# Hash products of the two column halves on the upper and the lower 64 rows of the array, with the projection laid out on the host

## The chip, the cores and the metric

The kernel is one program on one core of a Trainium2 chip. The metric is the device time of one execution in microseconds (us); the smaller the better. Engines are called PE (TensorE, the matrix array), DVE (VectorE), ACT (ScalarE), POOL (GpSimd) and SP (SyncE). DMA transfers are issued from the queues of SP, ACT and POOL.

## The reference

Three layers follow one another: a hash-bucketed attention (2 batches, 8 heads, 768 positions, head width 64), a top-2 mixture of 8 experts (1536 tokens, width 512, hidden width 1024) and a dense two-layer network (hidden width 2048). The change touches only the first. Cut to what matters:

```python
q_bits = (np.einsum('bhsd,dk->bhsk', q, proj) > 0)      # proj: 64 x 6
k_bits = (np.einsum('bhsd,dk->bhsk', k, proj) > 0)
mask = q_bucket[:, :, :, None] == k_bucket[:, :, None, :]   # bucket = the six bits as a number
scores = np.where(mask, scale * q @ k.T, -1e9)
attn = softmax(scores); out = attn @ v
```

Each position of q and k is multiplied by `proj`, the signs of the six products are its hash, and only positions with the same hash attend to each other.

## The kernel before, in words

The 16 heads are taken in 8 pairs (n = 0 to 7, j = 0 or 1 inside a pair). The host hands over q and k transposed, with the 64 rows of a head stacked twice, so that a tile `raw` (`rawq` and `rawk` in the profile) has 128 rows and 768 columns, and rows 64 to 127 repeat rows 0 to 63. The attention runs in 96 iterations g, 12 for each pair. In an iteration PE computes the scores of block g+2 (L277, `a_score`), DVE takes their maximum (L289, `a_soft`), PE transposes the probabilities of block g in two halves of three transposes (L319, `a_trans`), each half into one of two PSUM buffers of the tag "p", each half is copied out by ACT (L248) or DVE (L254), ACT computes the exponentials of block g+2 (L300, `a_exp`), and in every second iteration PE multiplies the transposed probabilities by v (L330, `a_av`). What else a pair needs is put into a table by iteration (`at`, and `at_m` for work that uses the single PSUM buffer of the tag "m"; `at_m` moves on to the next iteration in which no such work stands). Each engine runs its instructions in the order in which they are written out. Function `copy` chooses ACT or DVE for a copy by a ledger of the time that it has given to each.

The hash of a pair n >= 1 is `a_hash(n, hf)`, one call for each half of 384 columns, in two iterations: g0 - 2 and g0 - 1, where g0 is 7, 15, 29, 40, 50, 60 and 71 for n = 1 to 7 (the iterations come out as 5 and 6, 13 and 14, 27 and 28, 38 and 39, 48 and 49, 58 and 59, 69 and 70). A call makes four products (q and k of the two heads), each of `projq` (128 rows, of which rows 64 to 127 are zero, and 32 columns) with 384 columns of `raw`, into partitions 0, 32, 64 and 96 of the one "m" buffer. DVE then makes bits of them (L188) and scales half of these (L252, through `copy`). In iteration g0 `a_split` begins: ACT makes `u` (L169), POOL issues a transfer (L170) and subtracts (L171; on DVE for n = 1, j = 0), and so on for three more parts; `a_bits` then issues four transfers on POOL's queue (L197, L198) that bring the bits to the operands of the scores. `a_xt` (L364 to L375, a "m" user) transposes finished outputs, and the routing of finished tokens (`r_do`) is spread over iterations too. `w_conv` (L692 on ACT, L700 on POOL) prepares expert weights in iterations 28, 36, ... 68.

For pair 0 `z_hash(j)` does the same at the very start (L230), two products for each half, the second half in the buffer "av", and DVE reads the bits directly (L234).

`projq` is cleared by DVE and then filled by a transfer on POOL's queue (L65 to L68), which writes the six columns twice into rows 0 to 63. After it POOL issues `sgn`. ACT's queue carries `rawk` of head 0 at that time (L136), and ACT loads its table next (L494).

Of the kernel before, what the change touches and what calls it, by code (L numbers as in the profile page):

```python
# [9 lines left out]
F32 = mybir.dt.float32  # L10
F32R = mybir.dt.float32r
# [4 lines left out]
ALU = mybir.AluOpType  # L16
# [4 lines left out]
B, H, S, D = 2, 8, 768, 64  # L21
# [5 lines left out]
NB = 6  # L27
NROW = 24
HALF = 384
# [11 lines left out]
class Kernel:  # L41
# [19 lines left out]
    def consts(self):  # L61
        nc, a = self.nc, self.a
        p = self.cpool
        self.projq = self.t(p, [128, 32], F32, "projq")
        nc.vector.memset(self.projq, 0.0)  # L65
        src = a["proj"]
        src = bass.AP(tensor=src.tensor, offset=src.offset, ap=[[NB, 64], [0, 2], [1, NB]])
        nc.gpsimd.dma_start(self.projq[0:64, 0:2 * NB].rearrange("p (r b) -> p r b", r=2), src)  # L68
        self.sc = self.t(p, [128, 2], F32, "sc")
        nc.vector.memset(self.sc, 1.0)  # L70
        nc.vector.memset(self.sc[0:64, 0:1], SCALE)
        nc.vector.memset(self.sc[64:128, 1:2], SCALE)
        self.sgn = self.t(p, [128, 1], F32, "sgn")
        nc.gpsimd.dma_start(self.sgn, a["sgn"])
        self.ident = self.t(p, [128, 128], F32, "ident")
        make_identity(nc, self.ident)
# [97 lines left out]
            nc.scalar.activation(v1, k, AF.Copy, scale=self.sc[:, 1:2])  # L174
            eng.tensor_tensor(v2[0:64, :], k[0:64, :], v1[0:64, :].bitcast(F32), op=ALU.subtract)

    def a_hash(self, n, hf):
        nc = self.nc
        raw = self.raw[n]
        if hf == 0:  # L180
            self.hb[n] = self.t(self.ap, [128, S], F32R, "hb", 1)
        ps = self.t(self.ps_m, [128, HALF], F32, "m")
        cs = slice(hf * HALF, (hf + 1) * HALF)
        for i, (nm, j) in enumerate((("q", 0), ("q", 1), ("k", 0), ("k", 1))):
            nc.tensor.matmul(ps[32 * i:32 * i + 32, :], self.projq, raw[nm, j][:, cs],
                             start=True, stop=True)
        hb = self.hb[n][:, cs]
        nc.vector.tensor_scalar(hb, ps, 0.0, self.sgn[:, 0:1], op0=ALU.is_gt, op1=ALU.add)  # L188
        self.use(dve=0.47)
        self.copy(hb[64:128, :], hb[64:128, :].bitcast(F32), 0.4, 0.3, BIG)  # L190

# [30 lines left out]
    def z_hash(self, j):  # L222
        nc = self.nc
        u1, v1, u2, v2 = self.uv[0, j]
        pss = []
        for hf in range(2):
            cs = slice(hf * HALF, (hf + 1) * HALF)
            ps = self.t(*((self.ps_m, [128, HALF], F32, "m") if hf == 0 else (self.ps_a, [128, HALF], F32, "av")))
            for r, nm in ((64, "k"), (0, "q")):
                nc.tensor.matmul(ps[r:r + 32, :], self.projq, self.raw[0][nm, j][:, cs], start=True, stop=True)  # L230
            pss.append((ps, cs))
        def bits(h, d, r):
            ps, cs = pss[h]
            nc.vector.tensor_scalar(d[64:76, cs], ps[r:r + 12, :], 0.0, self.sgn[r:r + 12, 0:1], op0=ALU.is_gt, op1=ALU.add)  # L234
            if r == 0:
                nc.scalar.activation(d[64:76, cs], d[64:76, cs].bitcast(F32), AF.Copy, scale=BIG)

        for x in ((0, u2, 0), (0, v2, 64), (1, v2, 64), (1, u2, 0)):
            bits(*x)
# [251 lines left out]
    def attention(self):  # L491
# [3 lines left out]
        nc = self.nc  # L495
        LA = 2
        ps = self.t(self.ps_s, [128, 2, 512], F32, "s")
# [20 lines left out]
        self.at(0, self.a_load, 1)  # L518
        for n in range(1, NP):
            g = {1: 7, 2: 15, 3: 29, 4: 40, 5: 50, 6: 60, 7: 71}.get(n, 12 * (n - 1) - 2)  # L520
            h1 = self.at_m(g - 2, self.a_hash, n, 0)
            h1 = self.at_m(h1 + 1, self.a_hash, n, 1)
            self.at(g, self.a_uv, n)
            self.at(g, self.a_split, n, 0, 0)
            self.at(max(g, h1), self.a_bits, n)
            for x in range(1, 4):
                self.at(g + x, self.a_split, n, x // 2, x % 2)
            self.at(12 * n - 5, self.a_loadv, n)
            if n + 1 < NP:
                self.at(g + 4, self.a_load, n + 1)  # L530
# [16 lines left out]
        for bq, sc in ((0, 64), (1, 75)):  # L547
            g = xt[6 + bq] + 1
# [4 lines left out]
            g = self.at_m(g, self.r_do, bq, "rank", "place")  # L553
# [4 lines left out]
        for g in range(G):  # L558
            u, s, n, qh, j, c = self.dec(g)
# [748 lines left out]
def layout(inp):  # L1308
    import numpy as np
    c = np.ascontiguousarray  # L1310
    w64 = []
    w = c(inp["moe2_w_in"]).view(np.int64).reshape(4, 128, 2, 1024).transpose(2, 0, 1, 3).reshape(8, 128, 1024)
    w64.append(w)
    w = c(inp["moe2_w_out"]).view(np.int64).reshape(8, 2, 128, 512).transpose(0, 2, 1, 3).reshape(8, 128, 1024)
    w64.append(w)
    sgn = np.zeros((128, 1), np.float32)
    for g in range(4):
        for r in range(2 * NB):
            first = r < NB
            sgn[32 * g + r, 0] = -1.0 if first == (g >= 2) else 0.0  # L1320
    return {
        "qT": np.concatenate([inp["q"].transpose(0, 1, 3, 2)] * 2, axis=2),
        "kT": np.concatenate([inp["k"].transpose(0, 1, 3, 2)] * 2, axis=2),
        "v2": c(inp["v"].reshape(B, H // 2, 2, S // 128, 128, D).transpose(0, 1, 4, 3, 2, 5)).reshape(B, H // 2, 128, S // 128, 2 * D),
        "proj": inp["proj"], "sgn": sgn,
        "w_gate": inp["moe_w_gate"], "w_noise": inp["moe_w_noise"], "noise": inp["moe_noise"],
        "w1": inp["moe_w1"].reshape(E, 4, 128, FF),
        "w2": c(inp["moe_w2"].reshape(E, 4, 2, 128, DM).transpose(0, 1, 3, 2, 4)).reshape(E, 4, 128, 2 * DM),
        "w64": c(np.concatenate(w64)),
    }  # L1330
# [18 lines left out]
```

## Time and profile before

| | |
|---|---|
| median of 3 runs | 903.77 us (903.59 to 907.82) |
| profiled execution, its own time | 900.86 us |
| its span, first to last instruction | 899.1 us |
| mean granted clock of PE | 0.988 of full speed |
| attention | about 0 to 280 us of the span |

A profile shows one execution. Its page gives each engine's busy time; its chain of waits goes back from the last instruction to whatever released each step; the timeline lists instructions by start and duration, with the idle time before them and what ended it in square brackets. Full speed of PE is 2.4 GHz, the lower level 1.2 GHz. A full-precision product shows as two records, one behind the other.

### The profile page before, as it was taken

How to read it: one execution, taken by the hardware profiler on the slowest of the kernel's cores; microseconds unless marked ns; L12 is line 12 of the kernel's file. 1: busy time of each engine (PE TensorE's matmuls, PEld its weight loads, DVE VectorE, ACT ScalarE, POOL GpSimd, SP SyncE). 2: the span in 40 equal slices, each digit the busy share in tenths (PEclk: the TensorE clock that was granted, in tenths of full speed). 3: DMA queues.
4: the chain of work that ended last, by engine and by line, in shares of the span. 5: the costliest groups of instructions: out<-in, count | busy, mean ns of one | idle time of the engine just before them, and what ended most of it. 6: DMA issues, size and time to landing. Idle time of an engine off the chain costs nothing.

```text
span 899.1 us, 14065 instructions
## 1 busy us (share of the span) xinstructions
PE 867.4 (96%) x5409; PEld 747.7 (83%) x5409; DVE 539.3 (60%) x1079; ACT 439.4 (49%) x781; POOL 216.8 (24%) x222
## 2 busy tenths in 40 slices
PE   7999899989999999999999999999999999999997
PEld 4667666656667999999999999987989898989896
DVE  6676677897765568989898888837712121212120
ACT  5677777768774354435444343537614141414130
POOL 4142524565402300000000000005715050514040
PEclk9899999999999999999999999999999999999999
DMA  3428954744315756968787786748410101010000
GB/s 98 131 61 223 245 177 110 228 108 137 98 37 183 252 192 222 290 215 264 248 269 237 246 260 219 223 146 290 141 58 21 51 21 51 16 56 1 24 1 26
DMA packets 63016, 132.05 MB, mean 147 GB/s; under 512 B 8832, under 2 KB 25152, under 8 KB 62944
## 3 DMA queue, kind: packets, MB, share of 16 engines
q1 hardware_dynamic: 54240, 108.69, 37.9%
q0 software_dynamic: 7024, 20.38, 7.6%
q10 hardware_dynamic: 1680, 2.03, 0.7%
q8 instruction: 44, 0.72, 0.3%
q14 instruction: 28, 0.23, 0.1%
HBM read 91.90 MB, written 35.39 MB: 142 GB/s over the span
## 4 chain that ended last, share of the span: by engine, by line
PE 81%; DVE 6%; ACT 4%; DMA 4%; issue 2%; POOL 2%; SPq 0%; ACTq 0%; DVEq 0%; POOLq 0%
PE y L842 6%; PE y L844 5%; PE y L843 5%; PE g L1076 5%; PE g L1075 5%; PE g L1077 5%; PE av L330 5%; PE h L818 5%; PE h L819 5%; PE h L820 5%; PE o L1121 4%; PE o L1123 4%; PE o L1122 4%; PE s L277 4%; PE p L319 4%
## 5 line engine op out<-in xcount | busy, mean ns | idle before, releaser
L300 ACT ACTIVATE P<-s,sm 128x768 f32<-128x768 f32 x96 | 95.4, 994 | 35.0 <-DVE sm L291 29.5
L289 DVE TENSOR_REDUCE mx<-s 128x1 f32<-128x768 f32 x96 | 91.5, 954 | 24.7 <-PE s L277 23.7
L1085 POOL TENSOR_TENSOR gl<-sg,gh 128x512 fp32r<-128x512 f32 x48 | 67.2, 1400 | 162.1 <-ACT gh L1084 162.1
L277 PE MATMUL s<-v,u 76*128 76x384 f32 (+1 forms) x384 | 95.7, 371 | 5.8 <-ACT P L300 3.0
L1030 POOL DMA_INDIRECT yg<-ys,ysl x24 | 24.3, 1012 | 311.4 <-issue 309.1
L277 PEld LDWEIGHTS s<-v,u 76*128 76x128 f32 (+1 forms) x384 | 64.7, 195 | 35.8 <-issue 15.7
L319 PE MATMUL p<-ident,P 128*128 128x128 f32 x576 | 83.2, 280 | 10.4 <-DVE hh L254 4.5
L1081 DVE TENSOR_TENSOR sg<-g,sg 128x512 f32<-128x512 f32 x48 | 33.2, 691 | 91.1 <-ACT sg L1080 86.8
L319 PEld LDWEIGHTS p<-ident,P 128*128 128x128 f32 x576 | 70.0, 144 | 18.7 <-DVE hh L254 5.6
L330 PE MATMUL av<-PT,v 128*64 128x384 f32 (+1 forms) x216 | 74.7, 474 | 0.4 <-ACT xu L248 0.4
L825 ACT ACTIVATE hh<-h 128x416 fp32r<-128x416 f32 x56 | 29.1, 519 | 73.9 <-PE h L820 73.3
L842 PE MATMUL y<-hh,wh 128*128 128x416 f32 (+1 forms) x144 | 51.3, 356 | 0.0
L844 PE MATMUL y<-hh,wl 128*128 128x416 f32 (+1 forms) x144 | 49.8, 346 | 0.0
L843 PE MATMUL y<-hl,wh 128*128 128x416 f32 (+1 forms) x144 | 49.7, 345 | 0.0
L1080 ACT ACTIVATE sg<-g 128x512 f32<-128x512 f32 x48 | 28.7, 599 | 39.1 <-PE g L1077 36.7
L330 PEld LDWEIGHTS av<-PT,v 128*64 128x64 f32 x216 | 25.3, 138 | 25.5 <-issue 24.6
L248 ACT ACTIVATE PT<-p 128x384 f32<-128x384 f32 x80 | 35.5, 487 | 20.9 <-PE p L319 20.7
L1084 ACT ACTIVATE gh<-sg 128x512 fp32r<-128x512 f32 x48 | 30.3, 630 | 31.2 <-DVE sg L1081 30.2
L826 DVE SCALAR_TENSOR_TENSOR hl<-h,hh 128x416 fp32r<-128x416 f32 x56 | 32.9, 588 | 15.5 <-ACT hh L825 15.4
L1075 PE MATMUL g<-x2h,wh 128*128 128x256 f32 x144 | 40.1, 279 | 0.7 <-ACT x2h L1059 0.7
L1076 PE MATMUL g<-x2l,wh 128*128 128x256 f32 x144 | 40.0, 278 | 0.3 <-DVE x2l L1060 0.3
L1076 PE MATMUL g<-btl,wh 128*128 128x256 f32 x144 | 40.2, 279 | 0.0
(329 smaller groups left out, 2557.1 us busy)
## 6 DMA issues: line engine op xcount, KB each, us to landing
ws<-in_w SPq DMA_DIRECT2D x40, 512.0 KB, 5.0
d_in<-in_w SPq DMA_DIRECT2D x32, 512.0 KB, 5.2
bth<-in_w SPq DMA_DIRECT2D x16, 512.0 KB, 4.5
btl<-in_w SPq DMA_DIRECT2D x16, 512.0 KB, 4.4
wd<-d_o SPq DMA_DIRECT2D x32, 256.0 KB, 3.5
xs<-zt SPq DMA_DIRECT2D x8, 832.0 KB, 9.5
rawq<-in_qT SPq DMA_DIRECT2D x16, 384.0 KB, 4.5
rawk<-in_kT SPq DMA_DIRECT2D x15, 384.0 KB, 4.5
```

The source lines that it names most:

```text
L277: nc.tensor.matmul(ps[:, hf, :HALF], l[:kk, q0:q0 + 128], r[:kk, hf * HALF:(hf + 1) * HALF], start=st, stop=not st)
L289: nc.vector.tensor_reduce(mx, ps[:, :, :HALF], axis=AX.XY, op=ALU.max, negate=True)
L300: nc.scalar.activation(P, ps[:, :, :HALF], AF.Exp, bias=sm[:, 1:2], scale=sm[:, 0:1], accum_out=self.RS[u][:, c, j:j + 1])
L319: nc.tensor.transpose(ps[:, kb, :], P[:, hf, kb * 128:(kb + 1) * 128], self.ident)
L330: nc.tensor.matmul(self.AV[u, c][64 * j:64 * j + 64, :], self.vt[n][:, kb, 64 * j:64 * j + 64], self.PT[u, j][:, kb, cs], start=(kb == 0), ...
L818: nc.tensor.matmul(ps, wh[:, fs], xh[:, d, :n], start=(d == 0), stop=False)
L842: nc.tensor.matmul(ps, wh[:, ds_], hh[:, f, :], start=(f == 0), stop=False)
L843: nc.tensor.matmul(ps, wh[:, ds_], hl[:, f, :], start=False, stop=False)
L844: nc.tensor.matmul(ps, wl[:, ds_], hh[:, f, :], start=False, stop=(f == 7))
L1075: nc.tensor.matmul(ps[:, x, :], wh[:, fs], xh[:, d, :], start=(d == 0), stop=False)
L1076: nc.tensor.matmul(ps[:, x, :], wh[:, fs], xl[:, d, :], start=False, stop=False)
L1085: nc.gpsimd.tensor_tensor(gl[:, fo, :], g, gh[:, fo, :].bitcast(F32), op=ALU.subtract)
```

## The change

The host lays the projection out as a 128 x 32 array whose rows 64 to 127 hold the same values as rows 0 to 63. It is loaded by one transfer on ACT's queue; the clearing on DVE and the transfer on POOL's queue go. A product now takes 64 rows: the first half of the columns from rows 0 to 63, the second half from rows 64 to 127. All eight products of a pair are issued in one iteration (g0 - 1), the first half into an "m" buffer and the second half into a "p" buffer. DVE makes the bits of the second half in that iteration and those of the first half in the next, g0, before `a_split` and `a_bits`. In `z_hash` the four products of a head are issued with the halves alternating.

```diff
@@ consts
-        nc.vector.memset(self.projq, 0.0)
-        src = a["proj"]
-        src = bass.AP(tensor=src.tensor, offset=src.offset, ap=[[NB, 64], [0, 2], [1, NB]])
-        nc.gpsimd.dma_start(self.projq[0:64, 0:2 * NB].rearrange("p (r b) -> p r b", r=2), src)
+        nc.scalar.dma_start(self.projq, a["projq"])
@@ a_hash
-    def a_hash(self, n, hf):
-        nc = self.nc
+    def hash_mm(self, ps, r, hf, t):
+
+        rs = slice(64 * hf, 64 * hf + 64)
+        self.nc.tensor.matmul(ps[r:r + 32, :], self.projq[rs, :], t[rs, hf * HALF:(hf + 1) * HALF],
+                              start=True, stop=True)
+
+    def a_hash(self, n):
         raw = self.raw[n]
-        if hf == 0:
-            self.hb[n] = self.t(self.ap, [128, S], F32R, "hb", 1)
-        ps = self.t(self.ps_m, [128, HALF], F32, "m")
-        cs = slice(hf * HALF, (hf + 1) * HALF)
+        self.hb[n] = self.t(self.ap, [128, S], F32R, "hb", 1)
+        self.hps = [self.t(self.ps_m, [128, HALF], F32, "m"), self.t(self.ps_p, [128, HALF], F32, "p")]
         for i, (nm, j) in enumerate((("q", 0), ("q", 1), ("k", 0), ("k", 1))):
-            nc.tensor.matmul(ps[32 * i:32 * i + 32, :], self.projq, raw[nm, j][:, cs],
-                             start=True, stop=True)
-        hb = self.hb[n][:, cs]
-        nc.vector.tensor_scalar(hb, ps, 0.0, self.sgn[:, 0:1], op0=ALU.is_gt, op1=ALU.add)
+            for hf in range(2):
+                self.hash_mm(self.hps[hf], 32 * i, hf, raw[nm, j])
+        self.a_hb(n, 1)
+
+    def a_hb(self, n, hf):
+        nc = self.nc
+        hb = self.hb[n][:, hf * HALF:(hf + 1) * HALF]
+        nc.vector.tensor_scalar(hb, self.hps[hf], 0.0, self.sgn[:, 0:1], op0=ALU.is_gt, op1=ALU.add)
         self.use(dve=0.47)
         self.copy(hb[64:128, :], hb[64:128, :].bitcast(F32), 0.4, 0.3, BIG)
@@ z_hash
-            for r, nm in ((64, "k"), (0, "q")):
-                nc.tensor.matmul(ps[r:r + 32, :], self.projq, self.raw[0][nm, j][:, cs], start=True, stop=True)
             pss.append((ps, cs))
+        for r, nm in ((64, "k"), (0, "q")):
+            for hf in range(2):
+                self.hash_mm(pss[hf][0], r, hf, self.raw[0][nm, j])
@@ attention
-            h1 = self.at_m(g - 2, self.a_hash, n, 0)
-            h1 = self.at_m(h1 + 1, self.a_hash, n, 1)
+            h1 = g - 1
+            while {h1, h1 + 1} & self.busy:
+                h1 += 1
+            h1 = self.at_m(self.at_m(h1, self.a_hash, n) + 1, self.a_hb, n, 0)
             self.at(g, self.a_uv, n)
             self.at(g, self.a_split, n, 0, 0)
             self.at(max(g, h1), self.a_bits, n)
@@ layout (host)
+    projq = np.zeros((2, 64, 32), np.float32)
+    projq[:, :, :2 * NB] = np.concatenate([inp["proj"]] * 2, axis=1)
...
-        "proj": inp["proj"], "sgn": sgn,
+        "projq": projq.reshape(128, 32), "sgn": sgn,
```

## Rows read from the trace of the kernel before

**Rows 1.** Page: busy time of each engine, and shares of the chain that ended last.

```profile
PE 867.4 (96%) x5409; PEld 747.7 (83%) x5409; DVE 539.3 (60%) x1079; ACT 439.4 (49%) x781; POOL 216.8 (24%) x222
...
PE 81%; DVE 6%; ACT 4%; DMA 4%; issue 2%; POOL 2%; SPq 0%; ACTq 0%; DVEq 0%; POOLq 0%
```

**Rows 2.** Busy time by stretch (PE, PEld, DVE, ACT, POOL, clock, DMA share, GB/s).

```profile
290.00:899.00 609.00, 599.57 (x3651) 559.81 (x3649) 329.68 (x500) 235.72 (x373) 104.11 (x94) 1.00 0.45 149
```

**Rows 3.** Instructions of line L185: duration ns min/median/max, first and last start.

```profile
L185 PE MATMUL m<-rawq,projq x56: 483/487/510, 28.5 to 211.7; 128*32 128x384 f32 x56
```

**Rows 4.** Timeline of iteration 14, hash between transposes and scores (start us, us, ...).

```profile
55.23 0.82 PE L319 MATMUL p<-ident,P 128*128 128x128 f32 x6
...
55.76 0.87 ACT L248 ACTIVATE PT<-p 128x384 f32<-128x384 f32 x2 [1.61 <-PE p L319]
...
55.98 0.52 PE L185 MATMUL m<-rawq,projq 128*32 128x384 f32 x2
...
55.99 0.52 PE L185 MATMUL m<-rawk,projq 128*32 128x384 f32 x2
...
56.32 0.49 PE L185 MATMUL m<-rawq,projq 128*32 128x384 f32 x2
...
56.76 0.97 PE L277 MATMUL s<-v,u 128*128 128x384 f32 x4
56.90 0.62 DVE L188 TENSOR_SCALAR hb<-m,sgn 128x384 fp32r<-128x384 f32 x1
```

**Rows 5.** Timeline of iteration 8, transposes and scores with no hash between.

```profile
36.33 0.82 PE L319 MATMUL p<-ident,P 128*128 128x128 f32 x6
...
36.90 0.94 PE L277 MATMUL s<-v,u 128*128 128x384 f32 x4
```

**Rows 6.** Timeline of the start: projection, first hash product, first bits.

```profile
1.39 0.79 POOL L68 DMA_DIRECT2D projq<-in_proj  x1 [0.86 <-DVE sc L72]
...
7.43 0.51 PE L230 MATMUL m<-rawk,projq 128*32 128x384 f32 x1 [1.29 <-DMA projq<-in_proj]
...
8.34 0.61 DVE L234 TENSOR_SCALAR u<-m,sgn 12x384 fp32r<-12x384 f32 x1 [0.66 <-PE m L230]
```

**Rows 7.** Transfers issued in 0 to 30 us: size, median us to landing.

```profile
wg<-in_w_gate SPq DMA_DIRECT2D x2, 8.0 KB, 3.9
...
projq<-in_proj POOLq DMA_DIRECT2D x1, 3.0 KB, 6.0
```

**Rows 8.** Timeline around pair 1, iterations 5 to 9.

```profile
29.41 0.14 PEld L185 LDWEIGHTS m<-rawk,projq 128*32 128x32 f32 x2 [0.75 <-DMA rawk<-in_kT]
...
37.13 0.95 DVE L171 TENSOR_TENSOR u<-rawq,u 64x768 fp32r<-64x768 f32 x1 [2.04 <-ACT u L169]
...
39.90 1.31 PE L319 MATMUL p<-ident,P 128*128 128x128 f32 x6 [2.06 <-DVE PT L254]
```

**Rows 9.** Timeline of pair 4, first half of the hash.

```profile
122.05 0.52 PE L185 MATMUL m<-rawq,projq 128*32 128x384 f32 x2 [0.71 <-PE p L319]
```

**Rows 10.** Timeline of pair 6, maximum after the bits of both halves.

```profile
182.38 0.94 DVE L289 TENSOR_REDUCE mx<-s 128x1 f32<-128x768 f32 x1
```

**Rows 11.** Timeline of pair 3, scores that wait for bits.

```profile
108.91 0.98 PE L277 MATMUL s<-v,u 76*128 76x384 f32 x2 [2.50 <-DMA v<-hb]
```

**Rows 12.** Bits scaled on DVE (all, min/median/max ns), and one beside POOL's work.

```profile
L252 DVE TENSOR_SCALAR hb<-hb x14: 357/357/1065, 30.9 to 213.6; 64x384 fp32r<-64x384 f32 x14
...
209.12 2.37 POOL L700 TENSOR_TENSOR wl<-ws,wh 128x1024 fp32r<-128x1024 f32 x1 [2.75 <-PE av L330]
...
210.65 1.06 DVE L252 TENSOR_SCALAR hb<-hb 64x384 fp32r<-64x384 f32 x1
```

**Rows 13.** Busy time by stretch, columns as in rows 2: eight products with v.

```profile
41.20:44.00 2.80, 2.80 (x10) 0.81 (x9) 2.53 (x5) 0.60 (x3) 0.00 (x0) 0.52 0.30 41
```

**Rows 14.** Chain in order of time: eight products with v, twice.

```profile
41.21 2.76 PE av L330 x8
...
47.58 1.44 PE av L330 x8
```

More of the change, by code (lines that the diff above doesn't have):

```diff
@@ L175, in a_split @@
             eng.tensor_tensor(v2[0:64, :], k[0:64, :], v1[0:64, :].bitcast(F32), op=ALU.subtract)
-    def a_hash(self, n, hf):
-        nc = self.nc
-        raw = self.raw[n]
-        if hf == 0:
-            self.hb[n] = self.t(self.ap, [128, S], F32R, "hb", 1)
-        ps = self.t(self.ps_m, [128, HALF], F32, "m")
-        cs = slice(hf * HALF, (hf + 1) * HALF)
-        for i, (nm, j) in enumerate((("q", 0), ("q", 1), ("k", 0), ("k", 1))):
-            nc.tensor.matmul(ps[32 * i:32 * i + 32, :], self.projq, raw[nm, j][:, cs],
-                             start=True, stop=True)
-        hb = self.hb[n][:, cs]
-        nc.vector.tensor_scalar(hb, ps, 0.0, self.sgn[:, 0:1], op0=ALU.is_gt, op1=ALU.add)
+    def hash_mm(self, ps, r, hf, t):
[3 more added lines that the diff above has]
+    def a_hash(self, n):
+        raw = self.raw[n]
+        self.hb[n] = self.t(self.ap, [128, S], F32R, "hb", 1)
+        self.hps = [self.t(self.ps_m, [128, HALF], F32, "m"), self.t(self.ps_p, [128, HALF], F32, "p")]
+        for i, (nm, j) in enumerate((("q", 0), ("q", 1), ("k", 0), ("k", 1))):
+            for hf in range(2):
+                self.hash_mm(self.hps[hf], 32 * i, hf, raw[nm, j])
+        self.a_hb(n, 1)
+    def a_hb(self, n, hf):
+        nc = self.nc
+        hb = self.hb[n][:, hf * HALF:(hf + 1) * HALF]
+        nc.vector.tensor_scalar(hb, self.hps[hf], 0.0, self.sgn[:, 0:1], op0=ALU.is_gt, op1=ALU.add)
         self.use(dve=0.47)
```

## The prediction

> **What bounds the kernel now.** I read the page first, to see which engine sets the end. PE is busy for 96% of the span and holds 81% of the chain that ended last; DVE holds 6%, ACT and DMA 4% each [rows 1]. Then the busy time by stretch: from 290 us on PE works for 599.6 of 609 us at the full clock [rows 2]. Nothing of the change lies there, so whatever the attention gains or loses arrives at the end unchanged. Then the line of the hash: its products start between 28.5 and 211.7 us [rows 3], and those of pair 0 before that. Last the timeline around single hashes, because there PE, DVE and ACT take turns as the bound, and only the row tells which.
>
> A burst of four products looks like this: all four start within 0.01 to 0.02 us, their second records 0.34 us later, and the scores 0.78 us after the burst began [rows 4]. So products on different 32-column parts of the array already run side by side, and one burst costs PE 0.78 us, of which two records in sequence are about 0.68. Coming from transposes it costs more: the transposes take 0.75 us from their start to the hash (55.23 to 55.98, [rows 4]) and only 0.57 to the scores where no hash follows (36.33 to 36.90, [rows 5]), so 0.18 us is entering. A burst is worth 0.78 us behind products with v, and 0.96 behind transposes.
>
> **The change part by part.**
>
> *The start.* PE waits 1.29 us for the projection, until 7.43, and DVE then waits 0.66 us for the first product [rows 6]. The old transfer took 6.0 us to land; a small one on SP's queue took 3.9 [rows 7]. The new one, issued on ACT's queue behind `rawk` at about 1.3 us, should land between 5.2 and 7.3; I take about 6, because it no longer passes through POOL's queue, whose own issue took 0.79 us after a wait of 0.86 for DVE [rows 6]. DVE was free at 8.34 - 0.66 = 7.68, so the gain is at most 0.66 and at least 0.1; I take 0.6. What the transfer now stands ahead of, ACT's table load, is hidden by ACT's wait for the first q tile; the memset and POOL's issue disappear from idle engines; POOL's later constants come earlier. The layout on the host costs the chip only some KB more to load.
>
> *One burst instead of two, pairs 1 to 7.* The first burst of each pair goes. It stood behind transposes in pairs 1, 4, 5 and 6 and behind products with v in pairs 2, 3 and 7 (by the iteration numbers): 4 x 0.96 + 3 x 0.78 = 6.2 us. Two of these bursts also waited, 0.75 us for `rawk` in pair 1 [rows 8] and 0.71 for the "m" buffer in pair 4 [rows 9]: together 7.6 us. This counts the new burst of eight products at 0.78. No row shows two products on different rows of the array. The bounds: 0.78, if the row halves run beside each other as the column parts do, and 0.78 + 0.68 = 1.46, if they take turns. I take 0.78, because the nearest row is the column parts, whose starts lie 0.01 us apart. The Trainium skill (TensorE: Matmul & The Clock Gate, Part 3: Packing small matmuls) reports 16 tiles of 32 rows and 32 columns at once, 10.6 times as fast as one by one; by it the burst stays at 0.78. No run here shows it.
>
> *A new wait: the "p" buffer.* The second half's products must wait until the copy of the first transposed half is out. In pairs 1, 2, 3 and 7 the burst follows transposes directly; the two copies run from 55.76 for 0.87 us, so the first ends at 56.2, and the burst stood at 55.98 [rows 4]: 0.25 us each, 1.0 us. Behind PE then wait the next scores. In pairs 4 to 6 products with v (1.44 us, [rows 14]) cover it. The next transposes need the buffer back after DVE's 0.62 us (L188), which begins 0.92 us after the burst [rows 4]; those transposes' second half comes about 1.9 us after it, so this costs nothing unless DVE is late. Net so far 7.6 - 1.0 = 6.6 us.
>
> *The bits of the first half move two iterations later, to g0.* DVE has 0.62 + 0.36 us of work there that it had before in g0 - 2. `a_bits` and its four transfers on POOL's queue stay in iteration g0; they stand behind a transfer and a subtraction of POOL that wait for ACT's `u`, by when the bits are there. So the transfers are issued no later. In pair 1 the work falls into DVE's idle 2.04 us [rows 8], but for the same reason PE's gain there is not whole: ACT and DVE set the pace, PE waits 2.06 us for DVE anyway [rows 8]. Of the 0.96 + 0.75 - 0.25 there I count 0.9: minus 0.6. In pair 6 DVE is the bound: its maximum runs at 182.38, after the bits and routing work queued before it [rows 10]. The same work still stands before it afterwards (the first half's bits leave, the routing of block 0, which moves one iteration because `a_xt` of unit 6 goes from 50 to 51, comes in), and 0.6 us more follows in iteration 60. So the 0.96 is lost and 0.3 more: minus 1.3. In pairs 3 and 7 I take off 0.4 and 0.3, for a scaling on DVE that falls beside POOL's `w_conv` and for one that goes to ACT just ahead of `u`. Going through `copy`'s ledger for both orders, the scaling of the first half goes to ACT in pairs 6 and 7 and stays on DVE in the other five; the copies of transposes change by two in 192. `a_xt` of unit 0 moves from iteration 15 to 13 at no cost, the "m" buffer being free there.
>
> Sum: 6.6 - 0.6 - 1.3 - 0.4 - 0.3 = 4.0, with the start 4.6 us. The profiled execution took 900.86 us (899.1 span and 1.8 around it), so it would take 896.3; the median of the runs is 903.77, 2.9 above it, so the forecast there is 903.77 - 4.6 = **899.2 us**.
>
> **The rivals.**
>
> *Side by side, but given back.* PE waits 2.50 us at 108.9 for the bits of pair 3 [rows 11]. If that landing is set by other traffic and not by when POOL issues, all gained before it (0.6 + 0.9 + 0.5 + 0.1, about 2.1 us) turns into a longer wait: a gain of 2.5, 901.3 us. For it speaks that the transfer was issued 8 us earlier; against it that POOL's issue follows ACT, which comes earlier too. The Trainium skill (TensorEngine Tiling (Array Packing), PSUM Bottleneck) warns that tiling speeds up TensorE and not the reading of its results. By it every pair would go as pair 6 does, and only the start's 0.6 us would be left, 903.2 us. The trace agrees for pair 6 [rows 10] and not for pair 2, where ACT sat idle for 1.61 us until PE's transposes came [rows 4].
>
> *The row halves take turns.* Then seven bursts are 0.68 longer, 4.8 us: 4.6 - 4.8, 904.0 us, no change. For it: no row shows otherwise; against it: column parts overlap fully [rows 4].
>
> *DVE's scaling meets POOL (slower).* L252 takes 357 ns, but 1065 where POOL worked on L700 beside it, from 209.12 on [rows 12]. In g0 POOL starts its share of the pair. If each of the five scalings left on DVE waits for a POOL instruction of up to 2.37 us [rows 12] and PE for them, that is up to 11.9 us: 903.77 - 4.6 + 11.9 = 911.1. The change becomes slower than before from 0.9 us a scaling. Against it: POOL's first subtraction in g0 starts only after ACT's `u`, which is queued behind those bits.
>
> A stall of about 2 us also costs afterwards: behind the stall of [rows 8] the granted clock was 0.52 from 41.2 to 44.0 us, which is the lower of its two levels, 1.2 and not 2.4 GHz [rows 13], and eight products with v took 2.76 us and not 1.44 [rows 14]. One such spell more or less, 1.3 us and up, is inside the ranges below.
>
> **How the numbers follow.** The forecast has 0.62, given back 0.20, taking turns 0.10, slower 0.08. The forecast's own range goes from the gross 6.6 + 0.7 = 7.3 us of gain to 2.5: 896.5 to 901.3. The range for 8 in 10 takes in the cases of no change and leaves out the slower one and the far end: 896.5 to 904.5. This kernel's runs can tell about 0.5%, 4.5 us, from no change. The forecast lies just at that bound, so its 0.62 is divided: 0.42 faster. Same has the other 0.20, given back and taking turns: 0.50. Slower: 0.08.
>
> **What would show it.** Right: seven bursts instead of fourteen, in each the first records of all eight products within 0.1 us, and the scores 0.8 us after the burst began (1.0 where the "p" buffer is waited for); the first products start before 6.8 us and DVE's first bits at about 7.7; a wait of some 0.25 us of PE for a copy inside the bursts of pairs 1, 2, 3 and 7. Wrong: second-half products 0.3 us or more behind the first half's; L252 at about 1 us or above in five places; PE's wait at pair 3 longer by 2 us; a new stretch at the lower clock. The forecast fails if a stall of PE above 2 us appears or goes, which a shift of a few tenths of a us between POOL and DVE can do.

## The result, and the profile after

The change made the kernel slower by 0.7%: 910.0 us median (909.4 to 912.4, 9 runs) against 903.6 (899.9 to 907.8, 9 runs of the kernel before on the same chip), a ratio of 1.0071 with a 95% interval from 1.0052 to 1.0091. Forecast was 899.2. The profiled execution took 909.51 us, its span 907.8.

The page of the changed kernel, busy time and shares of the chain (beside [rows 1]):

```profile
PE 869.1 (96%) x5409; PEld 749.4 (83%) x5409; DVE 543.3 (60%) x1078; ACT 439.3 (48%) x781; POOL 218.0 (24%) x221
...
PE 83%; DVE 8%; DMA 3%; ACT 3%; issue 1%; POOL 1%; ACTq 0%; DVEq 0%
```

The totals hardly moved; a page does not show where 8 us went. So I laid the two traces side by side by one instruction that comes once in each of the 96 blocks, the maximum of the scores (L289 before, L294 after). Its start in the trace after, less that in the trace before:

| block | 0 | 1 | 8 | 22 | 34 | 38 | 48 | 53 | 54 | 55 | 56 | 58 | 95 |
|---|---|---|---|---|---|---|---|---|---|---|---|---|---|
| us | -0.64 | -0.03 | -3.03 | -3.37 | -4.56 | -2.85 | -3.85 | -5.14 | -3.27 | -1.98 | +2.05 | +3.30 | +5.42 |

At block 53 this trace is 5.1 us ahead, close to the 4.8 that the prediction's terms up to pair 5 add to. The closeness is partly luck: between blocks 1 and 8, with pair 1, it gains 3.0 us where 0.9 was counted, the start keeps 0.03 us of its 0.6, and between 34 and 38, at pair 3, 1.7 us are given back. At block 53 the five other traces with the new hash and no moved transfers (e1, e6, e9, e10 and e12 below) are 2.3 to 4.7 us ahead, and five with the old hash 0 to 3.2, so in the mean the new hash leads by 2.8 us. Between 53 and 58 (151 to 174 us) 8.4 us are lost at once.

**The hash itself.** Timeline of the changed kernel, pair 5's burst of eight products (beside [rows 4]):

```profile
146.70 0.51 PE L177 MATMUL m<-rawq,projq 64*32 64x384 f32 x1
...
146.75 0.51 PE L177 MATMUL p<-rawk,projq 64*32 64x384 f32 x1
147.04 0.48 PE L177 MATMUL m<-rawq,projq 64*32 64x384 f32 x1
...
147.50 0.97 PE L282 MATMUL s<-v,u 128*128 128x384 f32 x4
```

All eight first records start within 0.05 us, the second ones 0.34 later, the scores 0.80 us after the burst began: the 0.78 of the sum. Pair 6 looks the same (0.81). In the other five pairs the second product, the first one into the "p" buffer, waits for a copy, and the products behind it start with it. Timeline of pair 2:

```profile
53.22 0.51 PE L177 MATMUL m<-rawq,projq 64*32 64x384 f32 x1
53.55 0.51 PE L177 MATMUL p<-rawq,projq 64*32 64x384 f32 x1
...
54.35 0.97 PE L282 MATMUL s<-v,u 128*128 128x384 f32 x4
```

The second product starts 0.33 us behind the first in pairs 2, 3 and 7, 0.62 in pair 1 and 0.75 in pair 4, and these bursts take 1.13 to 1.56 us. The seven bursts take 8.0 us together; the fourteen before took 12.9, with the wait of pair 4. That is 4.9 us less, and 5.6 with the entering that the prediction counts for four of them, where its sum had 6.6.

Timeline of its start (beside [rows 6]):

```profile
6.55 0.48 PE L177 MATMUL m<-rawk,projq 64*32 64x384 f32 x1 [1.01 <-DMA projq<-in_projq]
...
7.70 0.61 DVE L239 TENSOR_SCALAR u<-m,sgn 12x384 fp32r<-12x384 f32 x1
...
11.00 1.80 POOL L224 TENSOR_TENSOR v<-rawk,v 64x768 fp32r<-64x768 f32 x1
11.35 1.67 DVE L213 TENSOR_SCALAR u<-rawq 64x384 fp32r<-64x384 f32 x1
```

DVE's first bits come 0.64 us earlier, and at block 1 the gain is gone: L213 now starts 0.35 us after POOL's L224 and ends 0.22 after it; before, it started 0.97 after POOL's and took 1.05.

**The loss.** Timeline of the changed kernel from 153 us, DVE's small operations and POOL's work (start us, us):

```profile
153.03 1.83 POOL L168 TENSOR_TENSOR u<-rawq,u 64x768 fp32r<-64x768 f32 x1
153.40 1.57 DVE L379 TENSOR_TENSOR lg<-lg,lt 128x96 f32<-128x96 f32 x1
...
156.88 1.82 POOL L172 TENSOR_TENSOR v<-rawk,v 64x768 fp32r<-64x768 f32 x1
157.07 1.70 DVE L414 TENSOR_TENSOR ls<-lg 128x48 f32<-128x48 f32 x1
...
161.50 2.37 POOL L707 TENSOR_TENSOR wl<-ws,wh 128x1024 fp32r<-128x1024 f32 x1
161.55 2.36 DVE L420 SCALAR_TENSOR_TENSOR rw<-ls,rw 128x24 f32<-128x24 f32 x1
...
163.82 1.79 POOL L172 TENSOR_TENSOR v<-rawk,v 64x768 fp32r<-64x768 f32 x1
163.94 1.72 DVE L421 TENSOR_TENSOR rw<-rw,nz 128x24 f32<-128x24 f32 x1
165.70 0.18 DVE L422 TENSOR_TENSOR rw<-rw,ls 128x24 f32<-128x24 f32 x1
...
167.58 0.90 PE L324 MATMUL p<-ident,P 128*128 128x128 f32 x3 [4.20 <-DVE PT L259]
```

Read start plus duration. L420 ends at 163.91, POOL's L707 at 163.87; L421 at 165.66, POOL's L172 at 165.61. These four operations take 0.18 to 0.26 us in the trace before; here each ends 0.04 to 0.11 us after POOL's: 7.4 us of DVE for work of 0.8. DVE's copies of transposes stand behind them, and PE waits 4.20 us. L379 belongs to `a_xt` (unit 6), the others to the routing of block 0. Both stand one iteration later than before (the slip), because pair 5's last bits now hold the "m" buffer in iteration 50, and `at_m` sends `a_xt` of unit 6 on to 51; there POOL's subtractions of pair 5 are under way.

Busy time by stretch there (PE, PEld, DVE, ACT, POOL, clock, DMA share, GB/s), changed kernel:

```profile
155.00:160.00 5.00, 3.47 (x16) 1.39 (x16) 4.75 (x9) 3.26 (x7) 4.59 (x7) 0.84 0.77 217
160.00:165.00 5.00, 3.38 (x17) 3.00 (x17) 4.97 (x7) 2.30 (x5) 4.92 (x3) 0.82 1.04 291
165.00:170.00 5.00, 2.42 (x9) 1.27 (x11) 4.07 (x14) 2.91 (x6) 0.62 (x1) 0.52 0.68 220
170.00:175.00 5.00, 5.00 (x30) 3.77 (x27) 2.14 (x10) 0.89 (x3) 0.00 (x0) 0.79 0.04 15
```

PE waits twice in these 20 us, 1.53 us until 157.21 and 4.20 us until 167.58, and the granted clock falls to the lower level, 1.2 GHz, after the first wait and again during the second. By the four means, of a level that counts as 1.0 or 0.5, that makes some 10 of the 20 us. Before it was at full speed in the same four stretches.

The Trainium skill (SBUF — State Buffer, Who interferes with whom) says that a VectorE instruction with two inputs in SBUF contends with a GpSimd instruction that reads SBUF, and that this contention is an exclusive lock on ports that the two share. The trace agrees: the four operations have two SBUF inputs, start behind POOL's and end with them, while the maxima, which read PSUM, keep their 0.94 to 0.96 us.

**Theories.** A: the loss comes from where the routing now falls, beside POOL's work. B, the rival: the new bursts, the "p" buffer and the bits in g0 cost by themselves.

### The profile page after: what moved, and what is told of

Its sections match the earlier page's. It is cut to its first block, busy times and chain, and to the rows that moved or that the text cites. A ratio compares the mean times of both kernels' runs of the same rounds, so it can differ in the third digit from the quotient of the medians.

```text
span 907.8 us, 14069 instructions
## 1 busy us (share of the span) xinstructions
PE 869.1 (96%) x5409; PEld 749.4 (83%) x5409; DVE 543.3 (60%) x1078; ACT 439.3 (48%) x781; POOL 218.0 (24%) x221
## 3 DMA queue, kind: packets, MB, share of 16 engines
q10 hardware_dynamic: 1824, 2.05, 0.7%
## 4 chain that ended last, share of the span: by engine, by line
PE 83%; DVE 8%; DMA 3%; ACT 3%; issue 1%; POOL 1%; ACTq 0%; DVEq 0%
PE av L335 7%; PE y L849 6%; PE s L282 5%; PE p L324 5%; PE y L851 5%; PE y L850 5%; PE h L825 5%; PE h L826 5%; PE h L827 5%; PE g L1082 4%; PE g L1083 4%; PE g L1084 4%; PE o L1130 4%; PE o L1128 4%; PE o L1129 4%; DVE mx L294 2%
## 5 line engine op out<-in xcount | busy, mean ns | idle before, releaser
L294 DVE TENSOR_REDUCE mx<-s 128x1 f32<-128x768 f32 x96 | 91.5, 953 | 27.1 <-PE s L282 21.8
L1037 POOL DMA_INDIRECT yg<-ys,ysl x24 | 26.2, 1091 | 310.6 <-issue 309.3
L324 PE MATMUL p<-ident,P 128*128 128x128 f32 x576 | 86.4, 286 | 13.8 <-DVE PT L259 6.2
L335 PE MATMUL av<-PT,v 128*64 128x384 f32 (+1 forms) x216 | 78.1, 492 | 0.4 <-ACT xu L253 0.4
L833 DVE SCALAR_TENSOR_TENSOR hl<-h,hh 128x416 fp32r<-128x416 f32 x56 | 32.9, 588 | 15.6 <-ACT hh L832 15.5
L1084 PE MATMUL g<-x2h,wl 128*128 128x256 f32 x144 | 40.5, 281 | 0.0
```

The costliest lines, as they stand in the source:

```text
L294: nc.vector.tensor_reduce(mx, ps[:, :, :HALF], axis=AX.XY, op=ALU.max, negate=True)
L324: nc.tensor.transpose(ps[:, kb, :], P[:, hf, kb * 128:(kb + 1) * 128], self.ident)
L335: nc.tensor.matmul(self.AV[u, c][64 * j:64 * j + 64, :], self.vt[n][:, kb, 64 * j:64 * j + 64], self.PT[u, j][:, kb, cs], start=(kb == 0), ...
L1084: nc.tensor.matmul(ps[:, x, :], wl[:, fs], xh[:, d, :], start=False, stop=(d == 3))
```

## The experiments

Each ratio is to the kernel before on the same chip in the same set. The ratio is that of the record and can differ from the quotient of the two medians by 0.001 or so. A time is compared only inside its set: the kernel before took 897.6 to 904.6 us in them.

| set | kernel | median us (runs) | before | ratio, 95% interval |
|---|---|---|---|---|
| 1 | e1 pair 5's burst earlier | 896.72 (12) | 897.82 | 0.9990 [0.9971, 1.0010] |
| 1 | e2 all bursts earlier | 899.13 (12) | 897.82 | 1.0016 [0.9999, 1.0033] |
| 1 | e3 slip alone, old hash | 907.17 (4) | 897.82 | 1.0099 [1.0067, 1.0131] |
| 1 | e4 one row half | 902.50 (12) | 897.82 | 1.0043 [1.0024, 1.0062] |
| 2 | e5 before again | 901.68 (1) | 898.41 |  |
| 2 | e6 routing moved | 901.32 (6) | 898.41 | 1.0040 [1.0025, 1.0055] |
| 2 | e7 routing moved, old hash | 899.56 (12) | 898.41 | 1.0013 [0.9998, 1.0028] |
| 2 | e8 load alone | 899.09 (12) | 898.41 | 1.0006 [0.9988, 1.0024] |
| 3 | e9 routing spread | 901.80 (12) | 904.62 | 0.9972 [0.9958, 0.9985] |
| 3 | e10 the same, with the slip | 905.56 (12) | 904.62 | 1.0001 [0.9981, 1.0021] |
| 3 | e11 the same, old hash | 901.95 (12) | 904.62 | 0.9961 [0.9943, 0.9980] |
| 3 | e12 e1 again | 903.85 (12) | 904.62 | 0.9994 [0.9972, 1.0015] |
| 4 | e13 e9, fills later | 896.24 (7) | 902.43 | 0.9926 [0.9904, 0.9948] |
| 4 | e14 e11, fills later | 898.58 (9) | 902.43 | 0.9957 [0.9932, 0.9982] |
| 4 | e15 e1, fills later | 898.30 (8) | 902.43 | 0.9939 [0.9919, 0.9960] |
| 4 | e16 before, fills later | 900.51 (12) | 902.43 | 0.9968 [0.9953, 0.9982] |
| 5 | e17 e15, load on POOL's queue | 893.80 (11) | 897.58 | 0.9947 [0.9929, 0.9965] |
| 5 | e18 e13, load on POOL's queue | 894.49 (12) | 897.58 | 0.9960 [0.9942, 0.9978] |

**The slip taken away, and the slip alone.** e1 moves pair 5's burst, e2 all bursts, one iteration up; e3 is the kernel before with `a_xt` of unit 6 one iteration later.

```diff
-            h1 = g - 1
+            h1 = g - 2 if n == 5 else g - 1          # e1;  e2: g - 2
```
```diff
-        xt = [self.at_m(73 if u == 9 else 6 * u + 13, self.a_xt, u) for u in range(13)]
+        xt = [self.at_m({6: 51, 9: 73}.get(u, 6 * u + 13), self.a_xt, u) for u in range(13)]   # e3
```

> The changed kernel, with the hash of pair 5 alone one iteration earlier (48 and 49), so that the transposed output of unit 6 stays in iteration 50 and the routing of token block 0 starts in 51, as before the change. Theory A (the loss is DVE's small routing instructions waiting beside POOL's subtractions of pair 5, because that routing slipped by one iteration): the 8 us lost between iterations 53 and 58 come back, L420 and L421 take about 0.2 us and not 2.4 and 1.7, and the time is 898 to 902 us. Theory B (the loss is in the new bursts, their wait for a transposes' buffer, and the bits moved to g0): no more than 1 us comes back, 908 to 910.

> The changed kernel with every pair's hash one iteration earlier: the eight products in g0 - 2, the first half's bits in g0 - 1, so that all other work stands in the iterations of the kernel before. Theory A: 898 to 902 us, as with pair 5 alone or 1 us better, since the first unit's transposed output goes back to iteration 15 too; PE waits about 1 us for rawk in pair 1. Theory B: 907 to 910, since bursts and buffers are the same.

> The kernel before, with one thing changed: the transposed output of unit 6 in iteration 51 and not 50, so that the routing of block 0 starts in 52. The hash is the old one. Theory A: the slip alone costs most of the 8 us, 907 to 912 us. Theory B: within 1 us of before, 902.5 to 904.5.

Timeline of e1, the same operations:

```profile
154.12 0.20 DVE L414 TENSOR_TENSOR ls<-lg 128x48 f32<-128x48 f32 x1
...
154.42 1.83 POOL L168 TENSOR_TENSOR u<-rawq,u 64x768 fp32r<-64x768 f32 x1
...
157.22 0.17 DVE L420 SCALAR_TENSOR_TENSOR rw<-ls,rw 128x24 f32<-128x24 f32 x1
157.43 0.19 DVE L421 TENSOR_TENSOR rw<-rw,nz 128x24 f32<-128x24 f32 x1
...
158.26 1.82 POOL L172 TENSOR_TENSOR v<-rawk,v 64x768 fp32r<-64x768 f32 x1
```

They now run in the gaps of POOL's work, at 0.17 to 0.20 us. Timeline of e3, two of them with the old hash:

```profile
164.44 2.36 POOL L700 TENSOR_TENSOR wl<-ws,wh 128x1024 fp32r<-128x1024 f32 x1
164.48 2.37 DVE L415 SCALAR_TENSOR_TENSOR rw<-ls,rw 128x24 f32<-128x24 f32 x1
...
166.76 1.79 POOL L175 TENSOR_TENSOR v<-rawk,v 64x768 fp32r<-64x768 f32 x1
166.88 1.72 DVE L416 TENSOR_TENSOR rw<-rw,nz 128x24 f32<-128x24 f32 x1
```

e1 and e2 are back at the time before, and e3 loses 1.0% with no new hash at all. Theory A holds for the loss; B does not explain it. But e1 and e2 gain nothing measurable either, where the sum said 4.6.

**One row half.** e4 is e1 with all products on rows 0 to 63:

```diff
-        rs = slice(64 * hf, 64 * hf + 64)
+        rs = slice(0, 64)
```

> As the first kernel of this call, but both column halves are multiplied on rows 0 to 63, so that two products share each part of the array and must take turns: two records, 0.68 us, more in each burst of the seven. If the row halves are what gives the gain: the burst takes 1.4 us and not 0.78, and the time is 3 to 5 us above that kernel's. If PE's time in the bursts is hidden behind ACT and DVE: within 1 us of it.

Timelines of pair 6, where no buffer is waited for, in e1 (first and last of the eight first records, and the scores):

```profile
175.26 0.51 PE L177 MATMUL m<-rawq,projq 64*32 64x384 f32 x1
...
175.31 0.51 PE L177 MATMUL p<-rawk,projq 64*32 64x384 f32 x1
...
176.07 0.97 PE L282 MATMUL s<-v,u 128*128 128x384 f32 x4
```

and in e4 (first product, first product of the second half, scores):

```profile
178.08 0.52 PE L177 MATMUL m<-rawq,projq 64*32 64x384 f32 x2
...
178.75 0.50 PE L177 MATMUL p<-rawq,projq 64*32 64x384 f32 x2
...
179.53 0.97 PE L282 MATMUL s<-v,u 128*128 128x384 f32 x4
```

The burst takes 1.45 us instead of 0.81, and pair 5's, which waits for its buffer in both, 1.76 instead of 1.12: 0.64 us more, where the rival of taking turns counted 0.68. The seven bursts together take 12.7 us instead of 8.0, 4.8 us more, and the kernel 5.8 us more by the medians, 4.7 by the means. So the row halves do run beside each other, and that is worth what the rival put on it.

**Routing out of POOL's way, first try, and the load alone.** e6 is e1, e7 the kernel before, each with the routing of blocks 0 and 1 put into iterations by hand; e8 is the kernel before with the new load only; e5 is the kernel before.

```diff
-        for bq, sc in ((0, 64), (1, 75)):
-            g = xt[6 + bq] + 1
+        for bq, (g, r, sl, sc) in enumerate(((57, 62, 66, 68), (65, 68, 69, 75))):
...
-            for nm in ("soft", "noisy", "top", "index", "pick"):
-                self.at(g, self.r_do, bq, nm)
-                g += 1
-            g = self.at_m(g, self.r_do, bq, "rank", "place")
-            self.at(g + 1, self.r_do, bq, "slots")
-            self.at(g + 2, self.r_do, bq, "weights")
+            self.at(g, self.r_do, bq, "soft")
+            self.at(g + 1, self.r_do, bq, "noisy", "top")
+            self.at(g + 2, self.r_do, bq, "index", "pick")
+            assert self.at_m(r, self.r_do, bq, "rank", "place") == r
+            self.at(sl, self.r_do, bq, "slots")
+            self.at(sl + 1, self.r_do, bq, "weights")
...
-                self.at(max(g + 2, sc) + i, self.r_scatter, bq, i)
+                self.at(sc + i, self.r_scatter, bq, i)
```

> The kernel before once more, for a trace from the same chip as the three that follow. Both theories expect the maxima of the attention at the times of its first trace within about 0.5 us, and the span near 899 us; a difference of 2 us or more would say that the curves of the earlier experiments, taken against a trace from another chip, are off by as much.

> The changed kernel with pair 5's burst one iteration earlier, and the routing of blocks 0 and 1 put by hand into iterations in which POOL has no tensor work of pair 5, pair 6 or the expert weights beside the small DVE operations. Theory A (routing operations of DVE that last as long as POOL's work beside them) expects the stretched ones at 153 to 200 us to go (about 5 us of excess), PE's wait behind them and the spell of lower clock with them, and the time 3 to 5 us below that of pair 5's burst moved alone: 892 to 895 us if that one is at 897. Theory B (the new bursts, the "p" buffer and the bits in g0 cost by themselves, wherever the routing stands) expects no more than 1 us below it.

> The kernel before with the same routing of blocks 0 and 1 by hand, and its own hash. Theory A expects it 1 to 3 us faster than the kernel before, since that one has a few clashes of its own (14.5 us of excess in all up to 300 us), and the change on top of it (the run with both) 3 to 5 us faster still, which would be the change's worth free of clashes. Theory B expects the difference between the two to be 1 us or less.

> The kernel before with nothing but the new load of the projection (the host lays it out with rows 64 to 127 at zero, one transfer on ACT's queue). The prediction counts 0.6 us of gain for it. Theory A expects DVE's first bits 0.6 us earlier, the subtraction after it stretched beside POOL's own (by 0.6 us, as in the changed kernel), and a change of the time between 0 and -0.3 us. Theory B, which blames the hash and not the clash, expects the whole 0.6 us at the end.

e5's maxima end 0.9 us later than in the first trace and are 1.8 us later at block 34, more than the 0.5 expected. Other traces scatter more: at block 38 five with the old hash (e3, e5, e7, e8, e11), whose schedule up to there is that of the kernel before but for e8's load, stand 0.1 to 3.2 us ahead of the first trace. So a curve of one execution is good to about 3 us only. e6 and e7 missed. Up to block 67 the maxima of e6 ran 8.3 us ahead of the trace before, 4.9 more than e1; by block 77 only 2.1. Timeline of e6 there:

```profile
204.23 2.36 POOL L706 TENSOR_TENSOR wl<-ws,wh 128x1024 fp32r<-128x1024 f32 x1 [10.19 <-issue]
204.25 2.38 DVE L455 CAST slot<-sf 128x6 int32<-128x6 f32 x1
```

I had moved block 1's slots beside POOL's weights: the same clash in a new place. e8 shows no gain of the start: first maximum 0.44 us earlier, second 0.17 later, 1.0006 in time.

**Second try, with and without the slip, with the old hash.** e9 is e1, e10 the changed kernel, e11 the kernel before, each with this table; e12 is e1.

```diff
+        for bq, (g, r, sl, wt, sc) in enumerate(((57, 62, 64, 65, 66), (64, 67, 68, 70, 75))):
...
+            self.at(wt, self.r_do, bq, "weights")
```

> Pair 5's burst one iteration earlier, block 0's routing in iterations 57 to 65 and block 1's in 64 to 70, so that no small operation of DVE stands in an iteration in which POOL subtracts for pair 6 or 7 or converts weights in iteration 68. The first try at this gained 4.9 us up to iteration 65 and lost 6.2 us in iterations 66 to 75, where block 1's slots fell beside POOL's weights (2.21 us of excess in one row). Theory A expects that loss to go: the maxima from iteration 75 on 3 to 5 us earlier than with pair 5's burst moved alone, and the time 2 to 5 us below it. Theory B, and the reading that DVE simply has too much work in these iterations, expect 1 us or less.

> The changed kernel as it is (pair 5's burst in iteration 49, its last bits in 50, the transposes of unit 6 in 51), with only the routing of blocks 0 and 1 put where the run beside it has it. If the 8 us come from where the routing falls (theory A), they are gone although the slip is still there: within 1.5 us of the run beside it. If it is the burst or the transposes in the later iteration themselves (theory B), the time stays 5 us or more above it.

> The kernel before, with its own hash and the routing of blocks 0 and 1 put where the two runs beside it have it. Theory A: faster than the kernel before by 1 to 4 us, and 3 to 5 us slower than the run with the new hash and pair 5's burst moved: that difference is the change's worth when neither meets POOL. Theory B: a difference of 1 us or less.

> Pair 5's burst moved alone, once more, on the chip of the three runs beside it. Its ratio was 0.999, with an interval from 0.997 to 1.001: theory A expects the same 0.997 to 1.001 again, theory B too; it is the measure for the others, and more runs of it tell a gain of 0.3% from none.

e9 is 2.0 us below e12, the low end of what A expected; but its maxima from block 75 on, expected 3 to 5 us earlier than in e12, come 0.8 us later in the traces, so where the 2.0 us are gained is not shown. e10 is back at the time before (1.0001) where the changed kernel lost 0.7%, but stays 3.8 us above e9, more than A allowed. Timeline of e10:

```profile
154.55 1.83 POOL L168 TENSOR_TENSOR u<-rawq,u 64x768 fp32r<-64x768 f32 x1
154.93 1.57 DVE L379 TENSOR_TENSOR lg<-lg,lt 128x96 f32<-128x96 f32 x1
```

`a_xt` itself is still in iteration 51, and its L379 still meets POOL: from block 53 to 56 e10 loses 3.1 us. And e11 decides against the other half of A: with routing out of the way, old and new hash measure alike. The gain is lost somewhere else.

**Pair 3.** There PE waits for the transfer of the bits. Timelines of the changed kernel, issue and use (beside [rows 11]), and of the issue before:

```profile
97.29 0.50 POOL L202 DMA_DIRECT2D v<-hb  x1
...
106.00 0.59 PE L282 MATMUL s<-v,u 76*128 76x384 f32 x2 [3.50 <-DMA v<-hb]
```
```profile
101.48 0.50 POOL L198 DMA_DIRECT2D v<-hb  x1
```

Both are the last of the pair's four transfers. Before, PE went on at 108.91: issued 4.2 us earlier, used 2.9 earlier. The other traces agree: from this issue to PE's scores it is 8.1 to 8.9 us in six traces with the new hash (the changed kernel, e1, e6, e9, e10, e12) and 6.6 to 7.4 in six with the old (the kernel before, e3, e5, e7, e8, e11). From block 34 to block 38 the traces with the old hash take 10.8 us in the mean (8.8 to 12.8, six traces), those with the new one 14.5 (13.9 to 15.6, six). So of the 4.5 us that the new hash is ahead at block 34 in the mean, 3.7 are given back here. The DMA engines are full throughout: a share of 0.92 to 1.08 in each 2 us from 90 to 106 in the changed kernel, part of it zero fills (`xs<-zt`, 832 KB each). The next four kernels move four of the eight fills: e13 is e9, e14 e11, e15 e1, e16 the kernel before, with

```diff
-            self.at(16 + 3 * e, self.zero_fill, e)
+            self.at({4: 45, 5: 47, 6: 55, 7: 57}.get(e, 16 + 3 * e), self.zero_fill, e)
```

> New hash, pair 5's burst one iteration earlier, routing spread as in the third set, and four of the eight zero fills (iterations 28 to 37) moved to iterations 45, 47, 55 and 57. If the gain is given back because the bits of pair 3 land late behind a full DMA, PE's wait there (3.15 us) goes to under 1 us, the maximum of iteration 38 comes 3 us earlier than in that run, and the time is 3 to 5 us below the old hash under the same conditions (the run beside it). If the landing does not depend on the zero fills, the wait stays at 2.5 us or more and the two runs measure alike again.

> The same zero fills and routing with the old hash: the measure for the run beside it. A full DMA as the cause: PE's wait at pair 3 (1.74 us) goes, and the time falls by no more than 2 us from 0.9961 of the kernel before, less than with the new hash. Otherwise no change from 0.9961.

> New hash with pair 5's burst moved and the four zero fills later, the routing where the changed kernel's own table puts it (0.999 of the time before without the moved fills). A full DMA as the cause: 3 to 4 us below that, 0.995 to 0.996. Otherwise 0.999 again. A clash of the routing with POOL can also move with it, so the trace's wait at pair 3 decides, and the time second.

> The kernel before with the four zero fills later and nothing else. A full DMA as the cause: its wait of 2.5 us at pair 3 goes, 1 to 2.5 us less time, 0.997 to 0.999, and the run of the new hash beside it 2 to 4 us below it. Otherwise 1.000.

Timeline of e13, PE at pair 3:

```profile
104.97 0.59 PE L282 MATMUL s<-v,u 76*128 76x384 f32 x2 [0.71 <-DMA v<-hb]
```

and of e16:

```profile
106.30 0.59 PE L277 MATMUL s<-v,u 76*128 76x384 f32 x2 [0.45 <-DMA v<-hb]
```

The wait falls from 3.0 to 3.7 us in six traces to 0.71 with the new hash (e15: 1.46), and from 1.0 to 2.5 us in five to 0.45 or nothing (e16, e14) with the old. Blocks 34 to 38 take 10.5 and 11.3 us with the new hash, 8.5 and 9.2 with the old: the new one still gives back 2 us, not 3.7. In time e15 is 2.2 us below e16 (means: 2.2 with an interval from 0.8 to 3.6) and e13 2.3 below e14 (means: 1.7, from -1.2 to 4.5), less than the 3 to 5 us expected of e13. So moving the fills shortens the wait, and the times speak for part of the gain being lost there. The traces do not show it come back: at block 34 the new hash leads by only 1.9 us in these four, and at block 38 by nothing. Nor is it fullness alone that counts, since the DMA share in e13 is still 0.96 to 1.18 in each 2 us from 94 to 106. e13 has the lowest ratio, 0.9926; the same table and fills with the old hash give 0.9957 (e14). Its profiled execution, 903.96 us, was the slowest of its seven, so only rows up to 110 us are used of it.

**After the attention.** From the last product of the experts' last layer to the second block of the dense stage the DMA moves up to about 410 GB/s and PE waits. This stretch takes 30.8 to 31.9 us in seven traces with the old load of the projection, 32.0 to 34.4 in ten with the new one, 33.0 in e8. e17 and e18 are e15 and e13 with the new layout's load on POOL's queue:

```diff
-        nc.scalar.dma_start(self.projq, a["projq"])
+        nc.gpsimd.dma_start(self.projq, a["projq"])
```

> New hash, pair 5's burst moved, zero fills later, and the projection (the same 128 x 32 array) loaded on POOL's queue instead of ACT's. If the queue of this load is what lengthens the stretch before the dense stage, it takes 31 to 32 us and not 32 to 34.4, and the time is 1 to 2 us below the run with ACT's queue (0.9939 of the time before), in spite of a first product some 0.5 us later. If not, the stretch stays near 33 us and the time at 0.994 or a little above.

> The fastest version so far (new hash, pair 5's burst moved, routing spread, zero fills later; 0.9926 of the time before) with the load of the projection on POOL's queue. By the queue as the cause 0.990 to 0.992 and a stretch of 31 to 32 us before the dense stage; otherwise 0.9926 to 0.994 and near 33 us.

The stretch takes 31.8 us in both, as the queue would have it, but the time did not fall (0.9947 and 0.9960, where 0.9939 and 0.9926 stood for ACT's queue). What lengthens the stretch stays open; it costs less than these runs can tell. The first product starts at 6.42 and 6.47 us and the first maximum at 10.38 and 10.29, no later than with ACT's queue (6.55 to 7.18 and 10.16 to 11.32 in ten traces): the 0.5 us of delay that was expected is not seen.

## Why the prediction was wrong, step by step

- **The step that failed** is in the paragraph on the bits: the routing of block 0 "moves one iteration because `a_xt` of unit 6 goes from 50 to 51". The prediction saw the move and counted only whose place it takes in DVE's queue in pair 6. What it took no price for is what runs beside the moved work: POOL's subtractions of pair 5 and its weights. That costs 8.4 us in the trace, about 9 us (1.0099) when done alone (e3), and undoing it brings 1.0071 down to 0.9990 (e1). The sum is blind to a moved step's neighbours on another engine. This is most of the 11 us between the forecast gain of 4.6 and the measured loss of 6.4; the points on pair 3, the start and the "p" buffer below hold what is known of the rest.
- **The rival on the slower side** (DVE's scaling meets POOL) had the right mechanism at the wrong operation. In the changed kernel the scalings were never met: 12 of them on DVE, 357 to 379 ns, against up to 1065 before [rows 12]. The price taken from [rows 12], up to 2.37 us for one meeting, is what L420 paid.
- **The rival "given back"** (the wait at pair 3) is right in kind. It supposed that the landing does not move with POOL's issue; it moved by 2.9 of 4.2 us in the changed kernel. The sum put nothing on this wait; in the mean 3.7 us more are spent there. With the slip undone the kernel stands at 0.999 (e1, e12, intervals from 0.9971 and 0.9972 upwards), where that rival (2.5 us of gain) put 0.9973. So its time is not excluded, and the forecast's 0.995 is.
- **The start**, 0.6 us: 0.64 at the first maximum of this trace, 0.03 at the second, nothing in time (e8). The 0.64 is luck as well: over ten traces with the load on ACT's queue (without e4, whose start takes turns too) the first maximum comes 0.2 us earlier in the mean than over seven with the old load, and the first product 0.5 us earlier. What ate it in this trace is DVE's L213 beside POOL's L224.
- **One burst instead of two at 0.78**: right where nothing is waited for, 0.80 and 0.81 in pairs 5 and 6. Taking turns costs 4.8 us in the bursts (e4), as counted.
- **The "p" buffer**, 1.0 us in four places: too small. PE stands idle for 1.7 us in five waits, by the summary of the hash line, and the second products start 2.4 us late in all. Pair 4, whose products with v were to cover the wait, has the longest, 0.75. "Second-half products 0.3 us or more behind", named as a sign against the forecast, is met in these five bursts for this reason and not because the halves take turns.

```profile
  ACT hh L253: 0.8, 2
  ACT PT L253: 0.7, 2
...
  ACT hl L253: 0.2, 1
```

- **Pairs 6 and 7** gain nothing, as counted: in e1 the maxima stand 3.3 us ahead at block 60, 3.4 at 66 and 3.5 at 95.
- **The end gets what the attention gains, unchanged**: not shown. In the changed kernel the last maximum comes 5.4 us later and the span is 8.7 us longer. Single executions differ by some us in the stretches behind the attention, and repeated runs of the kernel before by 6 to 12 us in each set. The intervals of e1 and e12 reach 2 us to either side, so 4.6 us would have shown and 1 us would not.

## What to carry to other kernels

When a change shifts a table of slots, list every step that moves and what each other engine does in the new place; here a small VectorE operation moved beside a GpSimd one lasted until that one ended, and everything queued behind it paid. Before counting a gain, find the next wait on a transfer: here, with full DMA engines, an issue 4.2 us earlier bought 2.9 us of landing. And do not take a curve of one execution for a gain. With the slip undone the change measures as no change (0.999). Only together with four moved fills does it show a gain of its own, 2.2 us (e15 against e16).

## What the runs showed of the hardware that was not expected

An operation of 0.18 us on 24 columns of SBUF took 2.36 us beside POOL's 2.37, thirteen times as long. Row halves and column parts overlap together: eight products of 64 rows and 32 columns start within 0.05 us, and the next scores follow 0.80 us after them, where four products of 128 rows and 32 columns took 0.78 [rows 4] and eight on one row half 1.45 (e4). And two waits of PE, of 1.53 and 4.20 us, went with a granted clock of 0.84, 0.82, 0.52 and 0.79 in four stretches of 5 us.
